# A new order for the first batch's list of steps in a sparse-attention and gated-MLP kernel

## The chip, the cores and the metric

The kernel runs on one core of a Trainium2 chip. The metric is the device time of one execution in microseconds (us), given as the median of three runs. TensorE is called PE here, VectorE DVE, ScalarE ACT, GpSimd POOL; SyncE (SP) does nothing but issue DMAs.

## The reference

For 8 batches of 576 tokens there are 8 attention heads of width 64. Heads 0 to 3 look at the last 32 tokens (local), heads 4 to 7 at every 32nd token back (strided). The heads side by side are x (576 x 512), which goes through a gated MLP:

```python
rel = pos[:, None] - pos[None, :]
mask_local = (rel >= 0) & (rel < stride)                        # stride = 32
mask_strided = (rel >= 0) & (pos[None, :] % stride == pos[:, None] % stride)
attn = softmax(where(mask, q @ k.T / sqrt(D), -1e9)); x = attn @ v
...
h = gelu_tanh(x @ w_in)                                         # 512 -> 1024
u, v = h[..., :512], h[..., 512:]
v_n = (v - mean(v)) / sqrt(var(v) + 1e-06) * g_ln
v_s = einsum('ts,bsd->btd', w_sg, v_n) + b_sg[None, :, None]    # over the tokens
out = x + (u * v_s) @ w_out
```

In the rest of the text "v" with a load or with a head is the attention's v; "the v product" and "the u product" are the two halves of `x @ w_in`.

## The kernel before, in words

**One list of words sets every order.** The kernel has some sixty small step functions. `emit` (L984) walks a string of words and calls one function for each; the class `InOrder` makes every engine run its instructions in the order in which they are issued, and every DMA queue too. A word is a step's name and a number: `SS-:3` is the strided scores of head pair 3. `-` marks the attention of the batch whose MLP is computed, a capital without a mark that of the next batch, `+` the one after it, small letters the MLP, `=` a step that belongs to no batch. `^` sends a step to the other choice of its kind (POOL or DVE, SP or ACT for a DMA, the other pair of PSUM buffers). The string `START` holds batch 0's list; `SECOND`, `LATER`, `CYCLE` and `LAST` hold those of batches 1 to 7.

**What batch 0 has to do beside its own work.** The products are run in two fp32r parts, high and low, so every weight has to be split on the chip. Weights come in 16 halves: 0 to 3 are the v half of `w_in` (one for each head pair of x, that is each 128 rows of the contraction), 4 to 7 the u half, 8 to 15 `w_out`. Each goes through `cl` load (SP), `ck` clip (POOL, `^` DVE), `cc` sign (DVE), `ca` field and `cd` rest (ACT), `ce` add (POOL), `cg` high part (ACT; `wih`, for `w_out` `woh`), `ch` low part (POOL, `^` DVE; `wil`, `wol`). The raw halves of `w_in` sit in the tile `stage`, which has five slots, those of `w_out` in `cs`; between the steps the numbers are in `cv` and `cx`. `w_sg` is transposed on PE in five pieces (`wl` load, `wt` turn, `wh` and `wm` split into `wsh` and `wsl`, `wst` for the last rows and the bias), and a tile `t` (`wo`, `wp`: memset by POOL, then cast by ACT) holds the ones that go with the bias.

**Attention of the first two batches.** `LP` (L439) loads rows of q and k of one head pair into one of four buffers (`rowq`, `rowk`); `TP` (L456) turns them with six PE transposes each, and `TC` (L467) copies the result out of PSUM on ACT (`qT`, `kT`). `SL` is the local scores of a head pair (`sa`, `sr`), `SS` the strided ones (`ss`). The softmax is `MK` mask (DVE), `MX` maximum (DVE), `SB` subtract (POOL, `^` DVE), `EX` exponential (ACT), `SU` sum (DVE), `ML` multiply (POOL, `^` DVE); x = 4 and 5 are the two parts of the local P (tile `sml`), 2 and 3 the strided pairs (`sms`). `PL`, `CL`, `CM` transpose the local P on PE (`ptl`) and copy it out; `VX`, `VY`, `VA` multiply by v (`ol`); `PS`, `CS`, `PV`, `PW` do the same for the strided pairs (`pts`, `os`). `XH` and `XL` write the two parts of x (`xt`), `XR` and `XD` send x out for the residual.

**The products.** `va` to `vd` are the four quarters of the v product for one pair of token tiles; quarter a needs x of head pair 0 and weight half 0, b pair 1 and half 1, and so on. The tail tokens (`v`), layer norm (`l.`), the u product (`u`), the spatial mix (`s`) and the output product (`o`) follow.

Of the kernel before, what the change touches and what calls it, by code (L numbers as in the profile page):

```python
# [22 lines left out]


START = """
cl=:1 LP-:3 cl=:0 LP-:0 TP-:6 mk= TC-^:6 ck=^:1 cl=:8 TP-^:7 cc=:1 ca=:1 mp= wo= wb= cl=:2 TC-:7 cd=:0
SS-^:3 TP-^:0 LZ-:0 cd=:1 TP-^:1 TZ-:0 ck=:0 ce=:1 LP-:1 LP-:2 cg=:1 ml=^ TC-:1 TC-:0 MK-:3 wc= cl=:9 MX-:3
SL-:0 SB-^:3 cl=:3 TP-^:2 ck=^:8 cc=:8 cc=:0 TP-:3 EX-:3 ch=^:1 wp= TZ-:1 ck=:2 MK-:4 SU-:3 MX-:4 TC-:2
SB-^:4 TP-:4 ck=:9 cc=:2 TC-:3 cl=:4 ML-^:3 SL-^:1 MK-:5 LZ-:1 MX-:5 cd=:9 EX-:4 ca=:0 SB-:5 TP-^:5 TC-:5
PS-:3 TZ:1 ce=:0 TC-:4 EX-:5 wd= LP:1 SU-^:4 SU-^:5 ML-:4 LP:0 ca=:2 SS-^:2 MK-^:2 cd=:2 ce=:2 ML-:5 TP^:2  # L30
wl=:1 TP^:3 TZ:0 cg=:0 MX-^:2 TC^:2 cd=^:8 TP:0 cd=:4 cd=:3 ch=:0 TC:3 PL-:5 CS-:3 LV-:0 ck=^:3 ck=^:4
wt=^:1 SB-^:2 CL-:5 cc=:9 cc=^:4 cc=:3 PL-:4 LV-:1 TC:0 EX-:2 TP^:1 cg=:2 CM-:5 ca=:9 CL-^:4 wh=:1 ce=:9
TC:1 VX-^:0 SU-:2 cl=:5 ca=:4 VY-:0 wm=^:1 LV-:3 ML-:2 XHb-:0 SL^:0 XHa-:0 ca=:8 cl=:6 PS-:2 cl=:7 we=^
LV-:2 XLb-:0 VA-:1 XLa-:0 ce=:4 va^:0 XR-:0 CS-:2 va:1 SL:1 XH-:1 XR-:1 XL-:1 vb:1 ca=:3 PV-:3 cd=:6 XD-^:0
MK:0 XD-^:1 ch=:2 PV-^:2 ck=:5 cc=:5 ce=:3 cg=:3 PW-^:3 PW-:2 cd=:5 cl=:13 cg=^:9 LP:3 ce=:8 cg=:4 cl=^:10
ca=:5 LP:2 ck=^:6 ch=:3 vb:0 XH-^:3 XH-:2 ck=^:7 ce=:5 cc=:6 MX:0 XL-:2 XL-:3 cd=:7 XR-:2 XR-:3 vc:0 vd:0
ch=:9 ca=:6 cc=:7 ch=^:4 lg= ce=:6 xt vc:1 LZ:0 cg=:5 cg=:6 cg=:8 g^:0 vd:1 ca=:7 ch=:6 cd=:10 SB^:0 g:1
ch=^:5 ce=:7 v^:2 vh XD-^:3 ls:0 XD-^:2 TP^:7 ls:1 TC:7 cg=:7 TP:6 ck=:13 TP:4 wl=:2 TC:4 vl ch=^:7 lr^:0
cc=:13 lm:0 TC:6 g:2 wl=:4 u^:2 rt LZ:1 u^:0 EX:0 SU:0 LV:0 cd=:13 wt=^:4 ug:2 wl=:0 lr:1 cl=:15 lm^:1 TP:5
lh:0 ll:0 ca=:13 TC:5 wh=:4 u^:1 ls:2 ce=:13 wm=:4 cg=:13 ck=^:10 lm:2 SS^:3 cc=^:10 LV:1 wt=:2 lr:2 MK:3  # L40
ug:0 wt=:0 SS^:2 wl=:3 u:3 ug:1 ca=:10 cl=:14 wh=:0 wh=:2 ML^:0 ce=:10 PL:0 wm=:0 lh^:1 lh:2 ug:3 cl=:11
wt=^:3 cl=:12 MK:2 ck=:15 wm=:2 cg=:10 ll:2 wh=:3 CL:0 ll:1 ch=:10 wm=:3 ck=:14 CM:0 cd=:14 s:1 cc=:14
ch=^:13 LQ+:0 ca=:14 ch=^:8 s:0 cc=:15 VA:0 MX:2 cd=:15 SB^:2 sm:0 ca=:15 VA:1 ce=:14 s:2 sm:1 ce=:15 cg=:14
ck=:11 sh:0 cd=:11 cd=:12 XH:1 cc=:11 MX:3 cg=:15 XL:1 ck=:12 TZ+:0 SB^:3 sh:1 sl:1 ca=:11 ch=:14 sm:2 LQ+:1
ch=^:15 cc=:12 ce=:11 XH:0 cg=^:11 sh:2 sl^:0 ca=:12 ch=^:11 s:3 o:2 sm:3 TZ+:1 XR:1 EX:2 o:0 r o^:1 o^:3
ce=:12 sh:3 sl:3 cg=:12 EX:3 sl^:2 SU:2 ch=^:12 o2:3 SU:3 ML:2 o2:2 PS:2 os:3 LV:2 od^:3 ML:3 XD:1 XL:0 os:2
CS:2 o2^:0 XR:0 LV^:3 LZ+^:1 od:2 PV:2 LV+:1 PW:2 LZ+:0 os:0 PS:3 o2:1 TQ+^:1 XH:2 XR:2 XD^:2 LQ+:2 CS:3
os:1 XD^:0 XL:2 TQ+:0 od^:1 LQ+:3 LV+:0 od^:0
"""
# [991 lines left out]
```

## Time and profile before

| | |
|---|---|
| runs | 555.96, 556.65 and 558.15 us; median 556.65 us |
| profiled execution | span 553.9 us from its first to its last instruction; the page gives no other time of it |
| busy | PE 533.6 us (96%), DVE 397.3, ACT 217.6, POOL 195.8 |
| mean granted clock of TensorE | 0.994 of full speed |

The busy share is a share of the span. PE is the engine to read: outside the first fifty microseconds it has next to no idle time, so a microsecond that PE waits there, or works at a lower clock, is a microsecond of the kernel. In the timeline a row is a run of like instructions: when the first started, how long until the last ended, and how long the engine had been idle before, with what it waited for.

### The profile page before, as it was taken

Reading aid. Unit: us, or ns where it says so; the run is one execution under the profiler, and the core shown is the slowest. Engines: PE = TensorE matmul, PEld = TensorE weight load, DVE = VectorE, ACT = ScalarE, POOL = GpSimd, SP = SyncE. Lnnn points to the kernel's source line nnn. Section 1 sums busy time; section 2 is a strip of 40 time slices with the busy share of each in tenths; the row PEclk is TensorE's granted clock in tenths of the full one; section 3 lists DMA queues with packets and bytes.
Section 4 is the critical chain, followed back from the end, with each engine's and each line's share of the span. In section 5 each row is a group of like instructions: output and inputs, shape, how many; then the busy total and the mean of one; then the engine's idle time right before and its main releaser. Section 6 shows DMA issues by size and latency. Waiting matters only on the chain.

```text
span 553.9 us, 17030 instructions
## 1 busy us (share of the span) xinstructions
PE 533.6 (96%) x7217; PEld 481.2 (87%) x7217; DVE 397.3 (72%) x707; ACT 217.6 (39%) x349; POOL 195.8 (35%) x376
## 2 busy tenths in 40 slices
PE   4869999999999999999999999999999999999997
PEld 3757899878998899988998899988998899988995
DVE  3875997568994499937995399945996399944532
ACT  4665885324440343323531244322631244322320
POOL 7765755404430153303440063302540053302310
PEclk9998999999999999999999999999999999999999
DMA  9898844768756755577446755577455760145002
GB/s 247 210 223 207 177 123 87 158 152 164 159 104 135 158 119 86 109 176 160 80 76 142 167 124 89 100 151 154 102 88 124 177 138 2 44 117 134 1 0 95
DMA packets 253677, 70.07 MB, mean 126 GB/s; under 512 B 237793, under 2 KB 239329, under 8 KB 253602
## 3 DMA queue, kind: packets, MB, share of 16 engines
...
## 4 chain that ended last, share of the span: by engine, by line
PE 85%; DVE 7%; POOL 2%; issue 2%; DMA 1%; SPq 1%; ACT 0%; POOLq 0%; DVEq 0%
PE sg L86 22%; PE o L86 18%; PE v L86 16%; PE u L86 16%; PE ol L86 3%; PE os L86 3%; PE pts L86 2%; PE sa L86 2%; PE ss L86 1%; PE ptl L86 1%; SPq L86 1%; DVE sms L86 1%; DVE cv L86 1%; DVE hv L86 1%; DVE sml L86 1%
## 5 line engine op out<-in xcount | busy, mean ns | idle before, releaser
L86 PE MATMUL sg<-wsh,vg 128*128 128x288 f32 x512 | 113.8, 297 | 0.2 <-DVE vg L86 0.2
L86 PE MATMUL u<-xt,wih 128*128 128x288 f32 x512 | 103.2, 297 | 0.0
L86 PE MATMUL o<-woh,vg 128*128 128x512 f32 x288 | 94.4, 397 | 0.0
L86 PEld LDWEIGHTS sg<-wsh,vg 128*128 128x128 f32 x512 | 85.6, 188 | 0.8 <-DVE vg L86 0.4
L86 PE MATMUL v<-wih,xt 128*128 128x512 f32 x256 | 83.0, 398 | 0.0
L86 PEld LDWEIGHTS u<-xt,wih 128*128 128x128 f32 x512 | 81.7, 188 | 0.7
L86 PE MATMUL u<-xt,wil 128*128 128x288 f32 x256 | 75.6, 295 | 0.4 <-DVE wil L86 0.4
L86 PE MATMUL sg<-wsl,vg 128*128 128x288 f32 x256 | 75.5, 295 | 0.0
L86 PEld LDWEIGHTS o<-woh,vg 128*128 128x128 f32 x288 | 54.1, 188 | 11.1
L86 DVE BATCH_NORM_STATS2 bnst<-hv 128x6 f32<-128x512 f32 (+1 forms) x40 | 27.0, 675 | 44.3 <-ACT hv L86 44.3
L86 PEld LDWEIGHTS v<-wih,xt 128*128 128x128 f32 x256 | 48.7, 190 | 10.5
L86 PE MATMUL o<-wol,vg 128*128 128x512 f32 x144 | 56.2, 390 | 0.0
L86 DVE TENSOR_TENSOR ob<-o,xn 128x512 f32<-128x512 f32 x32 | 20.9, 686 | 44.5 <-PE o L86 39.3
L86 PE MATMUL v<-wil,xt 128*128 128x512 f32 x128 | 50.4, 394 | 0.0
L86 PEld LDWEIGHTS u<-xt,wil 128*128 128x128 f32 x256 | 48.0, 188 | 0.7 <-DVE wil L86 0.7
L86 PEld LDWEIGHTS sg<-wsl,vg 128*128 128x128 f32 x256 | 48.2, 188 | 0.0
L86 ACT CAST vg<-gt 128x576 fp32r<-128x576 f32 (+2 forms) x48 | 22.9, 511 | 57.4 <-DVE gt L86 57.4
L86 ACT COPY pts<-pts 128x576 f32<-128x576 f32 x16 | 10.2, 640 | 74.6 <-PE pts L86 68.2
L86 DVE TENSOR_TENSOR gt<-sg,u 128x576 f32<-128x576 f32 x32 | 23.6, 743 | 19.7 <-PE sg L86 10.0
L86 POOL TENSOR_SCALAR va<-mv 128x2 f32<-128x2 f32 (+1 forms) x16 | 11.0, 687 | 74.4 <-DVE mv L86 74.4
L86 ACT ACTIVATE hv<-v 128x1024 f32<-128x1024 f32 x16 | 16.4, 1027 | 53.0 <-PE v L86 53.0
L86 PEld LDWEIGHTS o<-wol,vg 128*128 128x128 f32 x144 | 27.1, 188 | 4.9
...
## 6 DMA issues: line engine op xcount, KB each, us to landing
...
```

Of the source, the lines that this page charges most:

```text
L86: ins = self.tc.keep_in_program_order(op(*args, **kwargs))
```

## The change

The string `START` is replaced by another order of the same 405 words: none is added, none dropped, none changed, so each step keeps its engine, its queue and its buffers' kind. The other lists and all functions stay. Two lines of the 25 and what stands there now:

```diff
-cl=:1 LP-:3 cl=:0 LP-:0 TP-:6 mk= TC-^:6 ck=^:1 cl=:8 TP-^:7 cc=:1 ca=:1 mp= wo= wb= cl=:2 TC-:7 cd=:0
-SS-^:3 TP-^:0 LZ-:0 cd=:1 TP-^:1 TZ-:0 ck=:0 ce=:1 LP-:1 LP-:2 cg=:1 ml=^ TC-:1 TC-:0 MK-:3 wc= cl=:9 MX-:3
...
+mk= wb= LP-:3 TP-^:7 LP-:0 cl=:1 LP-:2 TP-:6 TP-^:1 TC-:7 TC-^:6 TP-^:0 TZ-:0 mp= wo= cl=:2 ml=^ SS-^:3 ck=:2
+MK-:3 LP-:1 wc= ck=^:1 TC-:1 MX-:3 TC-:0 cc=:1 SB-^:3 SL-:0 TP-:4 MK-:4 LP:0 cl=:3 MX-:4 TP-^:5 SB-^:4 cl=:0
...
```

In the listings below a name carries its batch, its head pair and a running number; where two listings are compared the running numbers differ and mean nothing.

On SP, from the start of the program, the loads stand like this before:

```order
L86 DMA stage_100<-in_moe_w_in_dram 128x2048
L86 DMA rowq_0_3_102<-in_q_dram 96x2x384
L86 DMA rowk_0_3_104<-in_k_dram 96x2x384
L86 DMA stage_100<-in_moe_w_in_dram 128x2048
L86 DMA rowq_0_0_107<-in_q_dram 96x6x64 x2
L86 DMA rowk_0_0_110<-in_k_dram 96x6x64 x2
L86 DMA cs_8_136<-in_moe_w_out_dram 128x1024
L86 DMA stage_100<-in_moe_w_in_dram 128x2048
L86 DMA rowq_0_1_219<-in_q_dram 96x6x64 x2
L86 DMA rowk_0_1_222<-in_k_dram 96x6x64 x2
L86 DMA rowq_0_2_225<-in_q_dram 96x2x384
L86 DMA rowk_0_2_227<-in_k_dram 96x2x384
```

and like this now:

```order
L85 DMA rowq_0_3_115<-in_q_dram 96x2x384
L85 DMA rowk_0_3_117<-in_k_dram 96x2x384
L85 DMA rowq_0_0_126<-in_q_dram 96x6x64 x2
L85 DMA rowk_0_0_129<-in_k_dram 96x6x64 x2
L85 DMA stage_100<-in_moe_w_in_dram 128x2048
L85 DMA rowq_0_2_133<-in_q_dram 96x2x384
L85 DMA rowk_0_2_135<-in_k_dram 96x2x384
L85 DMA stage_100<-in_moe_w_in_dram 128x2048
L85 DMA rowq_0_1_238<-in_q_dram 96x6x64 x2
L85 DMA rowk_0_1_241<-in_k_dram 96x6x64 x2
```

The rows of head pairs 3 and 0 have moved ahead of the first weights, those of pair 2 ahead of pair 1, and the load of `cs` is gone from the front. Further down SP's queue, the load of `w_sg` (whose buffer is the one that held the ones, so that it waits for ACT's cast of them) now has these rows around it; before it stood behind all loads of q and k rows, directly ahead of the loads of v:

```order
L85 DMA stage_100<-in_moe_w_in_dram 128x2048 x2
L85 DMA cs_8_322<-in_moe_w_out_dram 128x1024
L85 DMA wsg_1_331<-in_moe_w_sg_dram 128x576
L85 DMA rowq_1_1_402<-in_q_dram 96x6x64 x2
L85 DMA rowk_1_1_405<-in_k_dram 96x6x64 x2
L85 DMA cs_9_448<-in_moe_w_out_dram 128x1024
L85 DMA v_0_0_481<-in_v_dram 64x9x64
```

On PE, from the last turns ahead of the local P's transposes to the first matmuls of the v product, before:

```order
L86 MATMUL turnq_1_0_510<-ident_72,rowq_1_0_441 128x96 x6
L86 MATMUL ptl_0_4_523<-ident_72,sml_0_329 128x128 x4
L86 MATMUL ptl_0_8_528<-ident_72,sml_0_329 128x128
L86 MATMUL wsgT_1_539<-ident_72,wsg_1_493 128x128 x4
L86 MATMUL wsgT_1_539<-ident_72,wsg_1_493 64x128
L86 MATMUL ptl_0_0_551<-ident_72,sml_0_329 128x128 x4
L86 MATMUL turnk_1_0_564<-ident_72,rowk_1_0_444 128x96 x6
L86 MATMUL ol_0_0_581<-ptl_0_4_574,v_0_0_205 64x32 x32
L86 MATMUL ol_0_0_581<-ptl_0_5_546,v_0_0_205 64x32 x4
L86 MATMUL sa_1_631<-kT_1_0_502,qT_1_0_561 32x64 x36
L86 MATMUL pts_0_2_671<-ident_72,sms0_98 128x100 x8
L86 MATMUL ol_0_1_686<-ptl_0_5_546,v_0_1_393 64x32 x36
L86 MATMUL v_0_0_725<-wih_87,xt_95 128x512
```

and now:

```order
L85 MATMUL ptl_0_0_476<-ident_72,sml_0_298 128x128 x4
L85 MATMUL pts_0_3_487<-ident_72,sms1_99 128x100 x8
L85 MATMUL turnk_1_1_500<-ident_72,rowk_1_1_405 128x96 x6
L85 MATMUL ptl_0_4_536<-ident_72,sml_0_298 128x128 x4
L85 MATMUL ptl_0_8_541<-ident_72,sml_0_298 128x128
L85 MATMUL ol_0_0_547<-ptl_0_4_522,v_0_0_481 64x32 x32
L85 MATMUL ol_0_0_547<-ptl_0_5_545,v_0_0_481 64x32 x4
L85 MATMUL sa_1_613<-kT_1_0_474,qT_1_0_496 32x64 x36
L85 MATMUL ol_0_1_654<-ptl_0_5_545,v_0_1_389 64x32 x36
L85 MATMUL turnq_1_1_701<-ident_72,rowq_1_1_402 128x96 x6
L85 MATMUL v_0_1_725<-wih_87,xt_95 128x512
L85 MATMUL v_0_1_725<-wil_88,xt_95 128x512
```

The first part of the transposed P (`ptl_0_0`) and `w_sg`'s piece are ahead of the last one (`ptl_0_4`); the turn of batch 1's q of pair 1 (`turnq_1_1`) has come down between the second local P V and the v product; the strided transposes (`pts_0_2`) have gone from ahead of the v product to behind its first quarter.

On DVE, at the strided pairs' part of x, before:

```order
L86 SCALAR_TENSOR_TENSOR cv_5_843<-stage_100,cv_5_843 128x512
L86 TENSOR_SCALAR cv_6_808<-stage_100 128x512
L86 TENSOR_SCALAR cv_7_907<-stage_100 128x512
L86 SCALAR_TENSOR_TENSOR cv_6_808<-stage_100,cv_6_808 128x512
L86 TENSOR_REDUCE mx_1_0_911<-sml_1_815 128x18
L86 TENSOR_TENSOR xt_95<-os_0_2_826,xt_95 128x576
L86 TENSOR_TENSOR xt_95<-os_0_3_791,xt_95 128x576
```

and now:

```order
L85 TENSOR_REDUCE mx_1_0_851<-sml_1_791 128x18
L85 TENSOR_SCALAR cv_6_692<-stage_100 128x512
L85 TENSOR_TENSOR sml_1_791<-sml_1_791,mx_1_0_851 128x1152
L85 SCALAR_TENSOR_TENSOR cv_6_692<-stage_100,cv_6_692 128x512
L85 TENSOR_SCALAR cv_7_877<-stage_100 128x512
L85 TENSOR_TENSOR xt_95<-os_0_2_808,xt_95 128x576
L85 TENSOR_TENSOR xt_95<-os_0_3_853,xt_95 128x576
```

The low parts of x of pairs 2 and 3 (`xt<-os`) stand behind the clip of weight half 7 in both; the next batch's maximum and subtraction (`mx_1_0`, `sml_1`) have moved ahead of it, and the sign step of half 5 (`cv_5`) further up.

## Rows read from the trace of the kernel before

**Rows 1.** The page: PE busy; its tenths and clock in 40 slices
```profile
PE 533.6 (96%) x7217; PEld 481.2 (87%) x7217; DVE 397.3 (72%) x707; ACT 217.6 (39%) x349; POOL 195.8 (35%) x376
...
PE   4869999999999999999999999999999999999997
...
PEclk9998999999999999999999999999999999999999
```

**Rows 2.** Waits of PE, 50 to 140 us: total, times, longest
```profile
PE u L86 <- DVE wil L86: 0.4, 1, 0.4
PE os L86 <- DVE sml L86: 0.4, 1, 0.4
PE sg L86 <- DVE vg L86: 0.2, 1, 0.2
```

**Rows 3.** PE, timeline: start, us, operation, count [idle before it <-releaser]
```profile
6.56 1.19 PE L86 MATMUL turnq<-ident,rowq 96*128 96x96 f32 x6 [6.56 <-DMA rowq<-in_q_dram]
...
14.29 1.51 PE L86 MATMUL sa<-kT,qT 64*32 64x64 f32 x72 [1.27 <-ACT qT L86]
...
19.05 0.56 PE L86 MATMUL sa<-kT,qT 64*32 64x64 f32 x22
...
30.80 1.30 PE L86 MATMUL ptl<-ident,sml 128*128 128x128 f32 x5
...
34.70 0.66 PE L86 MATMUL turnk<-ident,rowk 96*128 96x96 f32 x6
35.54 1.25 PE L86 MATMUL ol<-ptl,v 64*64 64x32 f32 x72 [0.18 <-ACT ptl L86]
...
39.41 0.86 PE L86 MATMUL sa<-kT,qT 64*32 64x64 f32 x39 [1.50 <-issue]
40.20 1.59 PE L86 MATMUL pts<-ident,sms 100*128 100x100 f32 x8
41.72 2.15 PE L86 MATMUL ol<-ptl,v 64*64 64x32 f32 x72
43.80 0.79 PE L86 MATMUL v<-wih,xt 128*128 128x512 f32 x1
```

**Rows 4.** DMA queue q1 over 0:36.7 us: packets, MB, share of 16 engines
```profile
q1 hardware_dynamic: 16078, 8.18, 94.5%
```

**Rows 5.** SP, timeline of DMA issues: start, us of issuing
```profile
0.73 0.40 SPq L86 DMA_DIRECT2D stage<-in_moe_w_in_dram  x1
1.18 0.42 SPq L86 DMA_DIRECT2D rowq<-in_q_dram  x1
...
27.91 0.57 SPq L86 DMA_DIRECT2D wsg<-in_moe_w_sg_dram  x1
28.52 6.72 SPq L86 DMA_DIRECT2D v<-in_v_dram  x10
```

**Rows 6.** POOL, timeline: two steps on the local P
```profile
23.33 1.26 POOL L86 TENSOR_TENSOR sml<-sml,mx 128x640 f32<-128x640 f32 x1 [1.80 <-DVE mx L86]
...
28.59 1.26 POOL L86 TENSOR_TENSOR sml<-sml,sr 128x640 f32<-128x640 f32 x1
```

**Rows 7.** ACT, timeline: two casts and copies
```profile
14.84 0.62 ACT L86 CAST t<-ones 33x512 fp32r<-33x512 f32 x1
...
34.90 0.58 ACT L86 COPY ptl<-ptl 128x512 f32<-128x512 f32 x1 [0.44 <-PE ptl L86]
```

**Rows 8.** Windows by stage: us, busy by engine, granted clock, DMA share, GB/s
```profile
0.00:33.00 33.00, 21.35 (x356) 18.32 (x356) 23.07 (x44) 18.62 (x33) 23.82 (x44) 1.00 0.91 227
...
39.67:46.50 6.83, 6.83 (x123) 5.80 (x104) 1.47 (x3) 2.38 (x4) 4.07 (x4) 0.50 0.73 224
46.50:53.00 6.50, 6.11 (x214) 4.80 (x212) 3.85 (x10) 3.00 (x6) 2.75 (x3) 1.00 0.88 176
```

**Rows 9.** Tile stage, 0 to 60 us: duration ns min/median/max, first and last start
```profile
L86 POOL TENSOR_TENSOR cv<-cv,stage x7: 1282/1311/1699, 11.2 to 55.0; 128x512 int32<-128x512 int32 x7
L86 DVE TENSOR_SCALAR cv<-stage x5: 419/551/1499, 5.6 to 51.8; 128x512 f32<-128x512 int16 x5
```

More of the change, by code (lines that the diff above doesn't have):

```diff
@@ L25 @@
 START = """
-cl=:1 LP-:3 cl=:0 LP-:0 TP-:6 mk= TC-^:6 ck=^:1 cl=:8 TP-^:7 cc=:1 ca=:1 mp= wo= wb= cl=:2 TC-:7 cd=:0
-SS-^:3 TP-^:0 LZ-:0 cd=:1 TP-^:1 TZ-:0 ck=:0 ce=:1 LP-:1 LP-:2 cg=:1 ml=^ TC-:1 TC-:0 MK-:3 wc= cl=:9 MX-:3
-SL-:0 SB-^:3 cl=:3 TP-^:2 ck=^:8 cc=:8 cc=:0 TP-:3 EX-:3 ch=^:1 wp= TZ-:1 ck=:2 MK-:4 SU-:3 MX-:4 TC-:2
-SB-^:4 TP-:4 ck=:9 cc=:2 TC-:3 cl=:4 ML-^:3 SL-^:1 MK-:5 LZ-:1 MX-:5 cd=:9 EX-:4 ca=:0 SB-:5 TP-^:5 TC-:5
-PS-:3 TZ:1 ce=:0 TC-:4 EX-:5 wd= LP:1 SU-^:4 SU-^:5 ML-:4 LP:0 ca=:2 SS-^:2 MK-^:2 cd=:2 ce=:2 ML-:5 TP^:2
@@ L31 @@
[L31 to L45, printed above, removed]
@@ L46 @@
-ce=:12 sh:3 sl:3 cg=:12 EX:3 sl^:2 SU:2 ch=^:12 o2:3 SU:3 ML:2 o2:2 PS:2 os:3 LV:2 od^:3 ML:3 XD:1 XL:0 os:2
-CS:2 o2^:0 XR:0 LV^:3 LZ+^:1 od:2 PV:2 LV+:1 PW:2 LZ+:0 os:0 PS:3 o2:1 TQ+^:1 XH:2 XR:2 XD^:2 LQ+:2 CS:3
-os:1 XD^:0 XL:2 TQ+:0 od^:1 LQ+:3 LV+:0 od^:0
+mk= wb= LP-:3 TP-^:7 LP-:0 cl=:1 LP-:2 TP-:6 TP-^:1 TC-:7 TC-^:6 TP-^:0 TZ-:0 mp= wo= cl=:2 ml=^ SS-^:3 ck=:2
+MK-:3 LP-:1 wc= ck=^:1 TC-:1 MX-:3 TC-:0 cc=:1 SB-^:3 SL-:0 TP-:4 MK-:4 LP:0 cl=:3 MX-:4 TP-^:5 SB-^:4 cl=:0
+EX-:3 TC-:5 cl=:8 TP-^:2 wl=:1 TZ-:1 TC-:4 cd=:2 SS-^:2 wd= TP-:3 ca=:1 SU-:3 ML-^:3 MK-^:2 cd=:1 EX-:4 LZ-:1
@@ new lines @@
+wp= ce=:1 TC-:2 TC-:3 SU-^:4 MX-^:2 LP:1 cd=:3 SL-^:1 SB-^:2 cl=:9 TP^:1 MK-:5 TP:0 wt=^:1 ML-:4 TZ:0 PL-:4
+LZ-:0 cg=:1 cd=:0 ck=:0 PS-:3 TC:0 ck=^:8 TP^:3 TC:1 cd=^:8 MX-:5 SB-:5 ck=:9 LV-:0 cc=:2 EX-:2 EX-:5 cc=:0
+CL-^:4 we=^ ca=:0 SU-^:5 CS-:3 ck=^:3 ML-:5 ce=:0 cc=:9 PL-:5 cc=:3 cl=:4 CL-:5 VX-^:0 wh=:1 ca=:9 SU-:2 LV-:1
+CM-:5 cl=:6 ca=:3 VY-:0 cl=:5 TZ:1 cc=:8 cd=:4 ca=:2 TC:3 XHa-:0 wm=^:1 ca=:8 cg=:0 SL^:0 ce=:3 ch=^:1 cl=:13
+VA-:1 ck=^:4 cd=:6 cc=^:4 LV-:2 XHb-:0 ML-:2 XLa-:0 TP^:2 LV-:3 cd=:9 XH-:1 XR-:0 ch=:0 XLb-:0 TC^:2 ce=:8 cg=:3
@@ new lines @@
+XR-:1 ck=:5 va:1 ca=:4 XL-:1 PS-:2 cc=:5 ce=:2 CS-:2 SL:1 va^:0 MK:0 ch=:3 cg=:2 TZ+:1 vb:1 ca=:5 PV-^:2 cl=:7
+PW-:2 XD-^:0 XD-^:1 MX:0 PV-:3 ck=^:6 SB^:0 ce=:9 cg=^:9 ce=:4 cc=:6 XH-:2 ck=^:7 ch=:2 cd=:5 PW-^:3 cl=:11
+XH-^:3 lg= XL-:2 ca=:6 cd=:7 ch=:9 vb:0 XL-:3 EX:0 LP:3 XR-:3 ck=:13 cg=:4 cc=:7 ca=:7 cc=:13 vc:0 ce=:5 cg=:5
+ce=:6 cd=:13 SU:0 XR-:2 XD-^:3 vd:0 xt LZ:0 XD-^:2 ch=^:4 vc:1 g^:0 v^:2 wl=:4 vd:1 cg=:6 LP:2 ce=:7 cg=:7 TP^:7
+vh ch=^:5 ca=:13 ch=^:7 vl g:1 ls:0 TC:7 ch=:6 ce=:13 TP:6 u^:0 lm:0 lr^:0 TC:6 ug:0 g:2 cl=^:10 cd=:10 LZ+:0
@@ new lines @@
+wt=^:4 SS^:3 ls:1 u^:2 wl=:2 u^:1 lr:1 wl=:0 cg=:8 wt=:2 ML^:0 TP:4 ck=:11 wh=:4 wl=:3 lh:0 MK:3 ls:2 wm=:4
+wt=:0 lm:2 LV:0 ug:2 LQ+:1 cg=:13 ll:0 u:3 lm^:1 ug:1 ck=^:10 TC:4 TP:5 wh=:0 cc=^:10 wh=:2 lh^:1 cl=:15 PL:0
+wm=:0 ca=:10 ug:3 wt=^:3 TC:5 SS^:2 lr:2 CL:0 wm=:2 LZ:1 wh=:3 ll:1 ce=:10 wm=:3 cc=:11 ck=:15 lh:2 LQ+:0 ll:2
+MK:2 ca=:11 VA:0 TZ+:0 CM:0 MX:3 MX:2 SB^:3 cl=:12 SB^:2 cd=:11 cd=:15 s:1 EX:3 cl=:14 cg=:10 EX:2 ch=^:13 s:0
+cc=:15 ca=:15 cd=:12 ce=:15 LV:1 ce=:11 sm:1 sm:0 r SU:2 ck=:12 LQ+:3 s:3 ch=:10 cc=:12 ch=^:8 cg=:15 sh:1
@@ L49 @@
+cg=^:11 ck=:14 s:2 cd=:14 ch=^:11 ca=:12 sl:1 sm:3 sh:0 ch=^:15 ce=:12 VA:1 XH:1 XH:0 TQ+^:1 LV:2 sl^:0 sm:2
+cc=:14 ca=:14 o:0 ce=:14 sh:3 sl:3 o:2 XR:0 o^:1 ML:2 cg=:12 rt ch=^:12 SU:3 sh:2 o^:3 sl^:2 XL:1 XL:0 cg=:14
+ch=:14 ML:3 o2^:0 PS:2 o2:1 PS:3 CS:2 os:0 o2:2 XR:1 os:1 od^:0 PV:2 TQ+:0 os:2 XD:1 od^:1 LV^:3 od:2 PW:2
+LZ+^:1 o2:3 LV+:0 XD^:0 XR:2 os:3 od^:3 LV+:1 XH:2 CS:3 LQ+:2 XL:2 XD^:2
 """
```

## The prediction

> **What bounds the kernel now.** I read the busy line and the slices first [rows 1]: PE is busy for 533.6 of 553.9 us, and the only slices of PE below nine tenths at the front are the first four, some 55 us. So PE's work sets the end, and the change, which touches batch 0 alone, can win or lose only where PE waits or runs slowly in that head. The waits behind 50 us come next [rows 2]: in the 90 us from there PE waits 0.4 us for a weight's low part, 0.4 us for masked scores and 0.2 us for the mix's input. Everything behind the start of the v product is therefore one stream, and the time at which that stream starts goes into the span one to one. PE's own timeline [rows 3] gives that start: 43.80 us. The 43 us ahead of it hold four links: the first rows landing (6.56), the second local scores (19.05), the transposes of the local P (30.80) and the two local P V (35.54 and 41.72). The windows [rows 8] add a second limit: PE runs at half clock from 39.67 to 46.5 us, right where the v product begins. That is 0.50, the 1.2 GHz level; ahead of it the clock column reads 1.00, though the same six transposes take 1.19 us at 6.56 and 0.66 us at 34.70 [rows 3], so the engine itself was slow at the start too. Here I go by the durations.
>
> **The change, followed along the path.** What is counted is when the first matmul of the v product can run.
>
> First rows: before, 512 KB of weights and 288 KB of q must land ahead of the first transposes [rows 3, 5]; now the 576 KB of q and k of pair 3 must, since k is turned first. That is 224 KB less. Queue q1 moved 8.18 MB in 36.7 us [rows 4], 223 GB/s, so 1.0 us: 5.6 us instead of 6.56. Four sets of turns at up to 1.19 us and the first strided scores follow, and the first local scores come at about 11.2 us instead of 14.29.
>
> Second local scores: these come later, not earlier. Their rows stand behind another weight half and the rows of pair 2, and on ACT six conversions, casts and exponentials of some 0.6 us each (one of them is in [rows 7]) now stand ahead of the two copies they need. I walk to 21.7 us instead of 19.05, 2.7 us later.
>
> Softmax and transposes of the second local part: POOL's subtraction moves from 23.33 to about 26.0 us. Before, 5.26 us lay from its start to that of the multiply [rows 6], and one 1.3 us conversion add of POOL's stood among them; that add no longer does, so the multiply runs from 30.0 to 31.2 us and the transposes begin at 31.2 instead of 30.80. What was lost upstream is nearly paid back here.
>
> Local P V: before, 4.7 us lay between those transposes and the first P V, because the piece of w_sg and the other half of P came after them. Now both come before. What is left is 1.30 us of transposes, the 0.58 us copy [rows 3, 7] and some 0.2 us of handing over: 33.3 us instead of 35.54. The next batch's first scores wait for DVE's part of w_sg, to about 35.0 us, and take some 1.4. The second P V needs v of pair 1. As many bytes stand ahead of that load as before, and the queue was 94.5% busy to 36.7 us [rows 4], so reordering cannot bring it much forward: 36.2 to 37.8 us. P V takes 1.25 us at the upper level and 2.15 at the lower, the turn behind it 0.66 or 1.19 [rows 3]. The v product can start between 38.1 and 41.0 us. Its second matmul also needs the low part of half 0, which comes on POOL four operations of 1.15 to 1.3 us and their waits after the multiply, about 39.5 us. I take 39.5.
>
> So the terms are:
> - Start of the v product, 43.80 to 39.5: 4.3 us gained (2.8 to 5.7).
> - The strided transposes, 1.59 us at half clock [rows 3], move behind the first quarter. They still cost, at full clock 0.8 us: 0.8 lost from that lead.
> - The wait for masked scores (0.39) goes, since two quarters of v stand between the scores and the strided P V. If they did not cover DVE's masks it would be back: 0.4 lost.
> - The waits of the u product and the mix (0.4 and 0.2) go or stay; I count both, 0.6 gained (0 to 0.6).
> - Low clock: before, the 2.7 us of v product ahead of 46.5 us lost half of that, 1.35 us. If the clock still rises at 46.5, the product now spends 7.0 us at that level and loses 3.5: 2.15 lost.
>
> 4.3 − 0.8 + 0.4 − 2.15 + 0.6 = 2.35 us. The profiled span of 553.9 becomes 551.5. The median of the runs lies 2.75 us above that span (the runs spread over 2.2 us, and a span leaves out what lies around it); I carry that over: 556.65 − 2.35 = 554.3 us. With the bounds of the terms (start 2.8 to 5.7, u and mix 0 to 0.6) it is 552.9 to 556.4.
>
> **The clock term against the notes.** The rows show that PE was at the lower level from 39.67 to 46.5 us after the wait of 1.5 us at 39.41 [rows 3]. They do not show what ended it. The Trainium skill, "TensorE: Matmul & The Clock Gate", section "What's actually happening", says that "the default state is throttled, and activity releases the throttle". By that rule the release would follow the start of the v product, not the time of day, and the low stretch would move forward with it; the term of 2.15 us would fall away. It cuts the other way too: what precedes v still has waits, so the fall itself would not go.
>
> **Rivals.**
>
> The clock follows the work. If the low stretch moves forward by as much as the v product, its loss stays 1.35 us and the gain is 4.5: 552.1. If PE never falls, since the wait of 1.5 us at 39.41 [rows 3] goes, another 1.35: 550.8. For it: the 6.83 us of the window were PE's densest so far, and the rise came within them. Against: the new order has waits of its own at 35 and 36 us. I call this 551.5 us.
>
> POOL or the loads become the bound. POOL has eleven operations from the multiply at 31.2 us to the low part of half 2, by the multiply's 1.26 us [rows 6] 13.9 us, and I walk to 3.4 us of waits between them: 48.5 us. DVE's clip of half 7 reuses a buffer this frees, and the low parts of x of pairs 2 and 3 stand behind that clip; the third quarter waits for them. With 1311 ns as the median of the adds there is room of a microsecond. But the same add took up to 1699 ns and the same clip 419 to 1499 [rows 9]; 0.3 us more on each of eleven is 3.3 us, which leaves a gain of 0 to 1: 556. Against: before, PE had no such wait. The Trainium skill, "GPSIMD Engine Reference", section "1. Specifications", says that POOL shares its SBUF interface with DVE and that they contend when DVE reads two inputs; rows 9 show a spread of that kind, though not its cause.
>
> SP stands still: slower. The load of w_sg waits for ACT's cast of the ones, at 14.84 us before [rows 7] and some 20.6 us in my walk, since it is now behind an exponential and four conversions. Before, that load was issued at 27.91 us [rows 5], long after. Now rows of q and k, half of w_out, all of v of pairs 0 and 1 and a weight half stand behind it in SP's queue. As the queue holds little over, each microsecond that the cast is later than about 20 us makes v of pair 1, and with it the second P V and the v product, as much later. At 26 us it costs 5.5 us and eats the lead of 2.35: 559.8. The point from which it decides is a cast that ends after 23 us. For it: ACT is an in-order engine with four inputs from DVE and POOL ahead of that cast. Against: none of these waits lasts over 2 us in my walk.
>
> **How the numbers follow.** Forecast 0.45 at 554.3; clock with the work 0.2 at 551.5; POOL or DVE as bound 0.23 at 556; SP standing still 0.12 at 559.8. Half a per cent, about what a measurement of this kernel can tell from no change, is 2.8 us: faster means under 553.9, slower over 559.4. Forecast (its range holds 553.9) gives 0.18 of faster, the clock nearly all of its 0.2, the third case 0.01: 0.39. Slower is the greater part of the last, 0.09, and 0.02 of the third: 0.11. No change 0.50. The range leaves out the ends of the clock and of the SP case: 550.5 to 558.3.
>
> **What would show it.** In the changed profile the first transposes start at 5.6 us, the second local scores at 21 to 22, the last set of local transposes at 31, the two P V at 33 and 37, and the v product at 39 to 40; the granted clock is 0.5 until about 46.5. If it rises by 43, the second case holds. If PE waits within the v product for `xt` or `wil`, it is the third; if SP issues the load of w_sg after 23 us and PE waits for the second `v` load past 39, it is the fourth. My forecast is wrong if the v product starts after 41.5 us, or starts at 39.5 and the lead is gone by the u product.

## The result, and the profile after

| | before | after |
|---|---|---|
| runs, us | 556.42 (median of 4) | 562.99 (562.38 to 565.72, 4 runs) |
| profiled span, us | 553.9 | 560.9 |

The ratio of the runs is 1.0125, with a 95% interval of 1.0097 to 1.0153. The change makes the kernel slower by 1.25%, some 7 us. That is above the range given (550.5 to 558.3), and the side with the smallest chance.

The page after, in the lines that answer to [rows 1] (busy us by engine, tenths of PE and granted clock in 40 slices):

```profile
PE 535.2 (95%) x7217; PEld 482.3 (86%) x7217; DVE 405.1 (72%) x707; ACT 214.2 (38%) x347; POOL 195.8 (35%) x376
...
PE   5589899979999999999999999999999999999997
...
PEclk9658999999999999999999999999999999999999
```

The same 7217 matmuls cost PE only 1.6 us more, so some 5.4 of the 7.0 us are waits. DVE's same 707 instructions cost 7.8 us more: some of them have become slower. The clock is low in the second to the fourth slice, from 17 us on. The waits that PE has from 50 to 140 us, where [rows 2] had three with 1.0 us in all (and leave out a fourth, 0.69 us at `os` with no engine as its releaser):

```profile
PE os L85 <- ACT pts L85: 1.3, 1, 1.3
PE turnq L85 <- ACT hv L85: 1.2, 1, 1.2
PE pts L85 <- DVE xt L85: 1.0, 1, 1.0
PE v L85 <- DVE xt L85: 0.9, 1, 0.9
PE o L85 <- DVE ob L85: 0.8, 1, 0.8
PE o L85 <- DVE gt L85: 0.8, 1, 0.8
PE o L85 <- DVE wol L85: 0.3, 1, 0.3
PE sg L85 <- PE ol L85: 0.2, 1, 0.2
```

They come to 6.5 us, most of them put down to DVE. Two lie ahead of the u product (`v`, `turnq`); the others, but for the mix's 0.2, lie between 106 and 125 us, in batch 0's output product and batch 1's strided part beside it. The timeline of PE for the head, which answers to [rows 3]:

```profile
5.01 1.19 PE L85 MATMUL turnk<-ident,rowk 96*128 96x96 f32 x6 [5.01 <-DMA rowk<-in_k_dram]
...
11.21 1.51 PE L85 MATMUL sa<-kT,qT 64*32 64x64 f32 x72
...
22.00 0.56 PE L85 MATMUL sa<-kT,qT 64*32 64x64 f32 x22 [1.85 <-ACT kT L85]
...
28.42 1.30 PE L85 MATMUL wsgT<-ident,wsg 128*128 128x128 f32 x5 [2.78 <-DMA wsg<-in_moe_w_sg_dram]
...
34.08 1.11 PE L85 MATMUL ptl<-ident,sml 128*128 128x128 f32 x4 [1.21 <-POOL sml L85]
35.87 0.48 PE L85 MATMUL ptl<-ident,sml 128*128 128x128 f32 x1 [0.68 <-ACT ptl L85]
36.27 2.15 PE L85 MATMUL ol<-ptl,v 64*64 64x32 f32 x72
...
39.91 2.14 PE L85 MATMUL ol<-ptl,v 64*64 64x32 f32 x72
41.99 1.22 PE L85 MATMUL turnq<-ident,rowq 96*128 96x96 f32 x6
44.15 0.77 PE L85 MATMUL v<-wih,xt 128*128 128x512 f32 x1 [0.95 <-DVE xt L85]
```

The v product starts at 44.15 us, not at 39.5. The walk held up to the second local scores (22.00 us against 21.7). In this execution, set against the walk, 2.9 us were lost between there and the transposes of the second local P, which came at 34.08 instead of 31.2; another 1.8 were lost behind the second P V, which together with the turn runs at the lower level. What POOL and DVE did ahead of the transposes (POOL's two steps on the local P answer to [rows 6]):

```profile
28.32 1.63 POOL L85 TENSOR_TENSOR sml<-sml,mx 128x640 f32<-128x640 f32 x1 [0.95 <-DVE mx L85]
31.25 1.09 POOL L85 TENSOR_SCALAR cx<-cs 128x256 f32<-128x256 int16 x1 [1.30 <-DMA cs<-in_moe_w_out_dram]
32.77 1.26 POOL L85 TENSOR_TENSOR sml<-sml,sr 128x640 f32<-128x640 f32 x1 [0.43 <-DVE sr L85]
33.98 1.47 POOL L85 TENSOR_TENSOR cv<-cv,stage 128x512 int32<-128x512 int32 x1
```

```profile
27.13 0.38 DVE L85 TENSOR_SCALAR cx<-cs 128x256 f32<-128x256 int16 x1 [1.94 <-DMA cs<-in_moe_w_out_dram]
27.43 0.80 DVE L85 TENSOR_REDUCE mx<-sml 128x10 f32<-128x640 f32 x1
28.16 2.34 DVE L85 SCALAR_TENSOR_TENSOR cv<-stage,cv 128x512 f32<-128x512 int16 x2
...
34.23 1.77 DVE L85 SCALAR_TENSOR_TENSOR cv<-stage,cv 128x512 f32<-128x512 int16 x1
```

DVE's clip of weight half 8 stands ahead of the maximum of the local scores and waits 1.94 us for its load. POOL's clip of half 0 waits for its load too (1.76 us) and ends at 27.37, so the subtraction could not have started before that. It starts at 28.32 instead of 26.0, and the multiply behind it at 32.77 instead of 30.0. DVE's sign step, 0.69 us where nothing disturbs it, took 1.77 us beside POOL's add. Over the head the eight sign steps have a mean of 1190 ns; the same group before had 697 ns.

The windows by stage (columns as in [rows 8]) show DVE with next to no gap ahead of the v product (15.88 of 16.15 us), and the lower level of the clock throughout the stretch:

```profile
28.00:44.15 16.15, 12.85 (x250) 11.29 (x251) 15.88 (x24) 10.44 (x23) 11.81 (x10) 0.50 0.74 190
44.15:47.40 3.25, 3.25 (x10) 2.59 (x11) 2.78 (x3) 0.78 (x2) 3.25 (x3) 0.50 0.78 239
47.40:53.00 5.60, 5.60 (x170) 4.62 (x171) 3.91 (x8) 1.98 (x4) 5.51 (x7) 0.98 0.80 178
```

Where the 7.0 us of span are can be read from first matmuls in the two timelines:

| first matmul of | before, us | after, us | later by |
|---|---|---|---|
| v product | 43.80 | 44.15 | 0.35 |
| strided P V | 50.96 | 51.83 | 0.87 |
| u product | 63.26 | 66.15 | 2.89 |
| output product | 101.30 | 103.63 | 2.33 |
| batch 1's v product | 115.82 | 121.18 | 5.36 |
| its tail tokens | 127.99 | 134.69 | 6.70 |

So 0.35 us are ahead of the v product, 2.5 between it and u, and 4.1 behind the start of u (490.7 to the end before, 494.75 after).

### The profile page after: what moved, and what is told of

Read it like the earlier page. It is cut to its first block, busy times and chain, and to the rows that moved or that the text cites. A ratio compares the mean times of both kernels' runs of the same rounds, so it can differ in the third digit from the quotient of the medians.

```text
span 560.9 us, 17031 instructions
## 1 busy us (share of the span) xinstructions
PE 535.2 (95%) x7217; PEld 482.3 (86%) x7217; DVE 405.1 (72%) x707; ACT 214.2 (38%) x347; POOL 195.8 (35%) x376
## 4 chain that ended last, share of the span: by engine, by line
PE 84%; DVE 6%; DMA 3%; ACT 3%; SPq 1%; issue 1%; ACTq 0%; POOL 0%; DVEq 0%
PE sg L85 21%; PE u L85 18%; PE o L85 16%; PE v L85 16%; PE ol L85 3%; PE os L85 2%; PE ss L85 2%; PE sa L85 2%; PE pts L85 2%; DVE cv L85 2%; DMA rowk<-in_k_dram 2%; SPq L85 1%; DMA xd<-xs 1%; PE ptl L85 1%; DVE xs L85 1%
## 5 line engine op out<-in xcount | busy, mean ns | idle before, releaser
L85 POOL MEMSET v<- 32x128 f32 x16 | 3.2, 198 | 82.9 <-PE os L85 65.7
```

Of the source, the lines that this page charges most:

```text
L85: ins = self.tc.keep_in_program_order(op(*args, **kwargs))
```

## The experiments

Each kernel was timed against the kernel before on the same chip; a ratio above 1 is slower than before. Words in the diffs are those of `START`. "Control" is the changed kernel again (E14, below): 1.0089 [1.0071, 1.0108].

**E1 and E2: which half of the list costs?** E1 puts the old end behind the new head, E2 the new end behind the old head; the cut is at the first u words.

```diff
 E1: new list up to the first u word (without cl=:11 and TZ+:1)
-    new list from there
+    old list from there
 E2:
-    new list up to u^:0
+    old list up to u^:2
     new list from there
```

> The new order up to the first word of the u product (without the load of weight half 11 and one memset of the third batch), and behind it the remaining words in the old order. Theory (two separate losses: 2.9 us are lost by the start of the u product, because DVE and POOL are full with conversions there, and about 3.8 us behind it, because the rest of the list waits for DVE and ACT in the output stage): only the first loss is left, some 559.5 us, and PE's waits of 0.8 to 1.3 us in the output stage are gone. Rival (the waits of the output stage are the late head, handed on): they stay, some 562.5 us. Rival (the tail alone loses): as before, 556.4.

> The old order up to the first word of the u product, and behind it the remaining words in the new order. Theory (two separate losses): the second is left, 556.4 + 3.8 = 560.2 us, with the u product starting at 63 us as before and PE waiting in the output stage. Rival (the late head is handed on): 556.4, no such waits. Rival (the tail alone loses): 563.

E2 took 1.0101 [1.0073, 1.0128], some 5.6 us, with waits of the kind seen above. From u to the end it has 495.3 us, as after (494.75; before 490.7), so the end costs 4.7 us in this profile. The other 1.9 us of its span are ahead of u (65.20 us, before 63.26), in an execution of the old head that ran at the lower level to 49 us. E1 took 1.0143 [1.0121, 1.0164], but the place where the two lists meet has waits of its own (a turn waits 3.2 us at 68.44 for DVE's layer norm, another 1.4 for ACT), so its total says nothing of the head. It does show that the old end, run behind a late head, has none of the output stage's waits.

**E3: the head without w_out.** The conversion steps of `w_out` that the new head has go behind the u product's start.

```diff
-cl=:8 ... cl=:9 ... ck=^:8 ... cd=^:8 ... ck=:9 ... cc=:9 ... ce=:13 (21 words, among the steps of the head)
 u^:0
+cl=:8 cl=:9 ck=^:8 cd=^:8 ck=:9 cc=:9 ... ce=:13
```

> The new order, but all conversion steps and loads of w_out's halves (8 and up) that stand ahead of the u product are moved, in their order, to directly behind its first word. Five DVE instructions, seven of POOL and one wait for a load of w_out leave the head. Theory (DVE and POOL hold up the head: DVE is busy 15.9 of the 16.2 us ahead of the v product, its sign steps stretched from 0.7 to up to 1.8 us where POOL runs beside them): the last maximum of the local P ends near 26 instead of 28.2 us, the v product starts 1.5 to 3 us earlier than 44.15, the wait of 0.9 us in the third quarter shrinks. Rival (the low clock of PE sets the head): the v product starts within 0.5 us of 44.15. Rival (loads of v set it): the same. The total depends on what the moved steps cost behind u; no theory rests on it.

1.0318 [1.0286, 1.0349]. The v product started at 41.23 us, but the steps now held ACT and DVE ahead of batch 1's scores, and PE waited 10.8 us for `qT` at 76.86. Put there, the work costs more than it saves in the head; another place was not tried.

**E4 and E8: the two causes upstream.** E4 takes the waiting clip from ahead of the maximum, E8 gives POOL's steps on the second local P to DVE.

```diff
 E4:
-ck=^:8 TP^:3 TC:1 ... MX-:5 SB-:5
+TP^:3 TC:1 ... MX-:5 ck=^:8 SB-:5
 E8:
-ck=:0   SB-:5   ML-:5
+ck=^:0  SB-^:5  ML-^:5
```

> The new order with one word moved: DVE's clip of weight half 8 stands behind the maximum of the last part of the local P instead of ahead of it, so that DVE no longer waits 1.9 us there for the load of w_out. Theory (a chain of DVE and POOL work sets the head): the maximum ends at 26 instead of 28.2, but POOL's clip of half 0 runs to 27.4, so the subtraction comes 0.9 us earlier; of that 0 to 0.9 us reach the v product, 562.1 to 563. Rival (this wait alone is what made the head late): 2 us, 561.

> The new order with three steps moved from POOL to DVE, in their places: the clip of weight half 0 and the subtraction and multiplication of the last part of the local P. POOL loses 4.8 us of work ahead of the v product, DVE gets some 2. Theory (POOL and DVE together hold up the head, POOL's long instructions lying in the chain and stretching DVE's beside them): the last local transposes start at 32 to 33 instead of 34.08 us, the v product at 42 to 43 instead of 44.15, and the whole takes 561 to 562. Rival (DVE alone is full: 15.9 of 16.2 us): the v product starts 1 to 2 us later, 564 to 565. Rival (clock or loads): no change.

E4 took 1.0115 [1.009, 1.0139], transposes at 33.24 and the v product at 43.04; E8 took 1.0141 [1.0114, 1.0167], 33.14 and 43.47. Neither is better than the kernel after (1.0125) or the control, and links earlier by 0.7 to 1.1 us are less than the same head differs by from one execution to the next (E14, below). In E4 the maximum is done at 25.8 us, but POOL's clip of half 0, which waits 2.0 us for its load, holds the subtraction until 27.5: the waiting clip on DVE was only part of the delay. E8 is clear on one thing, the stretched sign steps. DVE, then POOL, in E8:

```profile
27.65 1.29 DVE L85 SCALAR_TENSOR_TENSOR cv<-stage,cv 128x512 f32<-128x512 int16 x2
...
38.45 3.47 DVE L85 SCALAR_TENSOR_TENSOR cv<-stage,cv 128x512 f32<-128x512 int16 x1
```

```profile
38.09 1.34 POOL L85 TENSOR_TENSOR sms<-sms,sr 100x576 f32<-100x576 f32 x1
39.39 1.29 POOL L85 TENSOR_TENSOR wil<-cv,wih 128x512 fp32r<-128x512 f32 x1
40.64 0.73 POOL L85 TENSOR_TENSOR cx<-cx,cs 128x256 int32<-128x256 int32 x1
41.34 2.40 POOL L85 TENSOR_SCALAR cv<-stage 128x512 f32<-128x512 int16 x1
```

The two signs that POOL no longer accompanies take 0.65 us each. The one at 38.45 met POOL's queue instead and ended at 41.92, after three of POOL's instructions had gone by. The collision was moved, not removed.

**E5 and E6: the cut elsewhere.** E5 keeps the new list to the first quarter of v, E6 the old list from the third mix on.

```diff
 E5: new list up to va:1
-    new list from there
+    old list from there
 E6: new list up to the third mix
-    new list from there
+    old list from there
```

> The new order up to the first quarter of the v product, the remaining words behind it in the old order. Theory (the front loses little by itself, since its v product starts at 44.15 against 43.80 us; the rest is lost by the order behind it): the u product starts at 64 to 64.5 us instead of 63.26, the output stage has none of the five waits, and the whole takes 557 to 558 us. Rival (the crowded front is what is paid for, by DVE and POOL work that it leaves undone): the u product starts at 65.5 or later and the whole takes 560 or more.

> The new order up to the third product of the spatial mix (without two loads or memsets of batch 2), the remaining words in the old order; the cut lies behind the u product, so that the seams of the first experiment fall away. Theory (the order of the output stage has waits of its own, 4.1 us less the 0.7 of before): the five waits of PE between 105 and 126 us are gone, the u product still starts near 66, and the whole takes 563 - 3.5 = 559.5 us. Rival (the waits are the late head handed on): they stay, 563.

E5 took 1.0027 [1.001, 1.0044]: the new front, with the strided transposes ahead of the v product as in the old list, costs 1.5 us. With E2's 1.01% that is 1.28%, about the whole loss, but the sum settles less than it seems: neither run has the new order between v's first quarter and u, where the profile after has its waits of 0.87 and 1.18 us, and against the control (1.0089) E2 alone is the whole loss. In E5's profile, one of the slowest of its 12 runs (560.84 us, median 558.38), u starts at 67.04 us, as the rival had it, while the median is near the theory's. E6 took 1.0217 [1.0195, 1.0239]: the output stage's waits are gone but for 0.3 us, but a load of v was issued too late at the seam and the local P V waited 5.35 and 1.61 us for it. It settles nothing. E9 joined E6 with E4 and E8 and waited there as well, 1.0199 [1.0177, 1.0221].

**E10, E11, E13 and E14: taking POOL out of DVE's way in the output stage.** E10 gives two gate multiplications to DVE; E11 also moves ACT's copy of strided P and a turn; E13 adds E4's clip and moves the clip of half 7 behind the low parts of x, which the third quarter waits for. E14 changes nothing.

```diff
 E10, E11, E13:
-sl^:0 ... sl^:2
+sl:0 ... sl:2
 E11, E13:
-TQ+:0 os:2 ... XH:2 CS:3
+os:2 TQ+:0 ... CS:3 XH:2
 E13 (and E4's line):
-XH-:2 ck=^:7 ch=:2 ... vb:0 XL-:3
+XH-:2 ch=:2 ... vb:0 XL-:3 ck=^:7
```

> The new order with two steps of the output stage moved from POOL to DVE in their places: the low parts of gated columns 0 and 2. They are the two POOL instructions beside which DVE's low parts of w_out took 1.48 and 1.95 us instead of 0.4. Theory (DVE's instruction is held until POOL's beside it is done): the two low parts of w_out take 0.4 us each again, DVE has 1.5 us of new work and 2.6 less of waiting, and PE's waits at 106, 111 and 113 us (0.8, 0.3, 1.0) shrink by about 1.2 in all: 561.8 us. Rival (DVE is simply full): those waits grow by 0.7 to 1.5 in all, 564 us. Rival (the stretched rows are an artefact of the record): durations stay.

> As the run before it, and two words moved in the output stage: ACT's copy of the strided transposes of pair 3 ahead of the high part of x of pair 2 (which waits for DVE and through it for a DMA's buffer), and DVE's turns of batch 2's first pair behind the third output addition. Theory (each wait of the output stage has its own cause in the order): the waits at 119.7 (0.8) and 125.3 (1.25) go as well, 2 us more than the run before it, 560 us. Rival (the waits replace one another): within 0.7 us of the run before it.

> The mended tail of the second run, with DVE's clip of weight half 8 behind the last local maximum and its clip of half 7 behind the low parts of x of pairs 2 and 3. Theory (the loss is the sum of named waits): 1.1 us of the head and 0.9 of the third quarter go on top: 558 us. Rival (the front's waits replace one another): 559.5 to 560.

> The new order unchanged, as the control for the run that follows on the same chip and as one more execution of its head (the v product started between 41.2 and 44.2 us in four executions of that same head). Any theory: 1.0 to 1.5% slower than the old order, with the five waits of the output stage at 0.8, 0.3, 1.0, 0.8 and 1.25 us. If the head's executions vary as widely as the runs so far say, the v product starts anywhere in 41 to 44.5 us and the waits are unchanged.

E10 took 1.0076 [1.0054, 1.0098], E11 1.0073 [1.0047, 1.0098], E13 1.0105 [1.0075, 1.0135], E14 1.0089 [1.0071, 1.0108]: no difference from the control that these intervals can tell. E14 is the kernel after once more, which took 1.0125 the first time: ratios 0.4% apart can belong to the same kernel. E14 also shows how much the head differs by itself: the same waits of the output stage, but the clip of half 8 found its load there and DVE's maximum began at 25.27 us, the transposes at 31.90 and the v product at 41.99. DVE's two low parts of `w_out` at the output stage, as groups of E10 and of the kernel after (count | busy us, mean ns):

```profile
L85 DVE TENSOR_TENSOR wol<-cxl,woh 128x256 fp32r<-128x256 f32 x2 | 1.7, 836 | 0.0
```

```profile
L85 DVE TENSOR_TENSOR wol<-cxl,woh 128x256 fp32r<-128x256 f32 x2 | 3.4, 1716 | 0.0
```

The same group had 388 ns before. The collision is half gone in E10 (0.41 and 1.26 us), and its wait with it, but PE now waits for the gates, since DVE makes them (waits of PE in E10):

```profile
PE o L85 <- DVE vg L85: 2.0, 2, 1.1
...
PE o L85 <- DVE ob L85: 0.8, 1, 0.8
```

In E13 the wait of the third quarter went and the turn behind it waited 2.2 us instead of 1.2.

**E15, E17 and E18: DVE's own order.** E15 moves the low part of half 15, turns and a store's transpose out of the way of what PE waits for; E17 adds to it three POOL steps given to DVE; E18 moves only the sign and field of half 12, which wait for a late clip, behind the gates.

```diff
 E15, E17:
-ch=^:15 ce=:12 VA:1 XH:1 XH:0 TQ+^:1 LV:2 sl^:0 sm:2
+ce=:12 VA:1 XH:1 XH:0 LV:2 sl^:0 sm:2 ch=^:15 TQ+^:1
 (XR:0 behind ch=^:12; E11's second pair of lines)
 E17:
-ML:2  sl^:0  sl^:2
+ML^:2 sl:0   sl:2
 E18:
-cc=:12 ... ca=:12 sl:1 sm:3 sh:0
+sl:1 sm:3 cc=:12 ca=:12 sh:0
```

> The new order with five words moved inside the output stage, no engine changed: on DVE the last gate multiplication ahead of the turns of batch 2's second pair and of a low part of w_out, the low part of half 12 ahead of a store's transpose, the third output addition ahead of the turns of batch 2's first pair; on ACT the copy of the strided transposes of pair 3 ahead of the high part of x of pair 2. Theory (PE's waits there come from what stands ahead on DVE and ACT): from the start of the u product to the v product of batch 1 it takes 53 to 53.7 us instead of 55.0 (52.6 in the old order), the waits at 106, 111 and 113 us go, and the whole is 2 to 3 us faster than the control. Rival (the waits replace one another, as when the two low gates went to DVE): 54.5 or more, within 0.7 us of the control.

> The tail order of the run with five moved words, and three POOL steps of the output stage on DVE in their places: the low parts of gated columns 0 and 2 and the multiplication of the strided P of pair 2. Beside these DVE's low parts of w_out took 0.97 to 2.73 us instead of 0.4. Theory (a DVE instruction that starts beside a POOL instruction is held until that one, and the next if it follows at once, has ended; that is what the output stage of the new order loses): the low parts take 0.4 us each although DVE has 2.2 us more of its own work, and from the start of the u product to the v product of batch 1 it takes 52.8 to 53.8 us (new order 55.0, five moved words 58.0, old order 52.6). Rival (DVE is too full there whatever runs beside it): 55 or more.

> The changed order with one sign step and one field step of w_out's half 12 moved behind the last gate multiplication. Theory (DVE's queue order in the output stage): DVE's sign of that half stood idle for about 2.5 us for POOL's clip, which itself waited for a late load, and the gate multiplications queued behind it. With the sign behind them the wait of 0.77 us at the output product goes, first u to batch 1's first v product takes 53.0 to 53.7 us instead of 55.0, and the kernel is 1 to 2 us faster than the unchanged new order (ratio to before 1.006 to 1.008, where that order had 1.009 and 1.0125). Rival (DVE is full there, and waits replace one another): the 0.77 us appears at another product, first u to batch 1's v stays at 54.5 us or more, ratio 1.009 or above.

E15 took 1.0155 [1.0133, 1.0176]. The wait for the gate's input is gone, but the low part now starts in the midst of two POOL instructions (DVE, then POOL, in E15):

```profile
107.18 2.73 DVE L85 TENSOR_TENSOR wol<-cxl,woh 128x256 fp32r<-128x256 f32 x1
```

```profile
106.59 1.68 POOL L85 TENSOR_TENSOR sms<-sms,sr 100x576 f32<-100x576 f32 x1
108.24 1.39 POOL L85 TENSOR_TENSOR vg<-gt,vg 128x576 fp32r<-128x576 f32 x1
```

It ended at 109.91, 0.28 us after the second of them, and PE waited 1.7 us for it. In E17 those POOL steps are DVE's, and the same instruction is short (DVE, then POOL, in E17):

```profile
108.99 0.41 DVE L85 TENSOR_TENSOR wol<-cxl,woh 128x256 fp32r<-128x256 f32 x1
```

```profile
108.78 1.21 POOL L85 TENSOR_TENSOR wol<-cxl,woh 128x256 fp32r<-128x256 f32 x1 [1.00 <-ACT woh L85]
```

POOL is not idle beside it: a low part of its own had started 0.21 us earlier, and this time POOL's instruction was the long one (1.21 us; 0.73 in E10). The clean case is the low part of half 15. It took 1.48 us at 102.53 in the kernel after, beside POOL's gate multiplication, and 0.41 us with POOL idle, in E10 (99.62) and in E17 (104.43). So POOL is what stretches it. E17 differs from E15 by those three steps alone and took 1.008 [1.0056, 1.0105], with the intervals apart: in E15's order the collision cost time. Against the control it won nothing: PE waited 1.9 us for a gate that DVE made late, and u to batch 1's v took 54.5 us, between the theory (up to 53.8) and the rival (55). E18 took 1.0091 [1.0063, 1.0119]; the wait of 0.77 us for `gt` became one of 0.91 us for POOL's `vg`, and u to batch 1's v took 55.1 us, as in the kernel after (55.0). That is what the rival said: the waits replace one another.

**E12 and E16: one step in the old list.** E12 is the kernel before with DVE's copy of the last transposed piece of the local P moved ahead; E16 adds the high and low part of half 7 moved forward.

```diff
 E12, E16 (old list):
-CL-:5 cc=:9 ... cg=:2 CM-:5
+CL-:5 CM-:5 cc=:9 ... cg=:2
 E16:
-vh ... ls:1 TC:7 cg=:7 ... ch=^:7
+cg=:7 vh ... ch=^:7 ls:1 TC:7
```

> The old order with one word moved: DVE's copy of the last transposed piece of the local P ahead of three sign steps (1.7 us) that stood in front of it. PE waits 0.96 us for that copy at 34.21 us before. Theory (a chain of DVE work sets the start of the v product in the old order too): that wait goes, both local P V and the v product come up to 1 us earlier, 0.1 to 0.2% faster than before. Rival (v of pair 1 or the waits behind set it): no change.

> The old order with the copy of the last piece of P first, as in the run that was 0.22% faster, and with ACT's high and DVE's low part of weight half 7 moved ahead of the second layer-norm statistics. In that run the u product waited 1.69 us for this low part, which ended at 65.3 as in the old order, so that the earlier v product was given back there. Theory (a chain of conversions on ACT and DVE is a floor under the u product): the wait goes, 0.4 to 0.5% faster than the old order, some 554 us. Rival (something else then holds the mix or the layer norm): as the run with one move, 0.2%.

E12 took 0.9978 [0.9964, 0.9992], E16 0.9973 [0.9955, 0.9991]: both are faster than the kernel before, by about a quarter of a per cent, in 12 runs each; E16 is not told apart from E12. E12 also tests the statement that the start of v goes into the span one to one. Its v product starts 3.0 us earlier than before. Most of that is not the copy's. The wait of 0.96 us for it went, but PE then waited 1.30 us for ACT's copy, and the first local P V came 0.45 us later than before. Behind it the wait of 1.50 us at 39.41 [rows 3] is gone, and PE was at the upper level from 33.2 us on (the second P V took 1.25 us instead of 2.15). This is what the stream made of it (PE in E12):

```profile
40.81 0.50 PE L85 MATMUL v<-wih,xt 128*128 128x512 f32 x1
...
44.85 0.73 PE L85 MATMUL v<-wih,xt 128*128 128x512 f32 x2 [1.90 <-issue]
```

and its waits from 40 us:

```profile
PE v L85 <- issue: 1.9, 1, 1.9
PE u L85 <- DVE wil L85: 1.7, 1, 1.7
```

PE lost 1.9 us in the product itself and 1.7 us at u, waiting for `wil`; at the mix nothing of the lead was left (83.31 us against 83.33). The wait of 1.9 us has no releaser on record, like the one of 1.50 us that stood ahead of the product before; it may be the same wait in another place, which was not tested. The profile, of a slow execution (556.53 us, median 555.48), does not account for the gain of 1.3 us in the runs. In E16 the wait for `wil` is gone and the mix starts at 82.51.

## Why the prediction was wrong

**The step that failed first is "Everything behind the start of the v product is therefore one stream, and the time at which that stream starts goes into the span one to one."** It was read from the waits of the old order [rows 2], but the list `START` runs on to the end of batch 0 and all of it was put in a new order. The prediction costed no step behind the mix. From the start of u on, the new order takes 4.1 us more in the profile, by waits between 106 and 125 us, and the new end by itself costs 1.01% in the runs (E2). The statement is also false inside the old order: in E12 a lead of 3.0 us at the v product had become 1.3 at the u product (61.98 against 63.26) and nothing at the mix. Two readings that this step rests on were short: only the first three slices of PE are below nine tenths, not four, and [rows 2] leave out the wait of 0.69 us at 112 us.

**The second was the lead, "I take 39.5".** It was a walk along single durations, and two things in it failed. The waits for loads ahead of the subtraction were not in it, DVE's clip of half 8 and POOL's of half 0: where these loads are late, as in the kernel after, the transposes are 2.9 us late, and still 2.0 with the clip of half 8 out of the way (E4). Where they are in time, the walk holds up to there, and still the v product is 2 us later than 39.5. PE, in E18, whose head is that of the kernel after:

```profile
31.60 1.11 PE L85 MATMUL ptl<-ident,sml 128*128 128x128 f32 x4 [1.18 <-POOL sml L85]
...
33.80 2.15 PE L85 MATMUL ol<-ptl,v 64*64 64x32 f32 x72
...
39.74 1.22 PE L85 MATMUL turnq<-ident,rowq 96*128 96x96 f32 x6
41.67 0.76 PE L85 MATMUL v<-wih,xt 128*128 128x512 f32 x1 [0.71 <-ACT qT L85]
```

The P V take 2.15 us and more, the turn 1.22, where 1.25 and 0.66 are those of the upper level: the prediction named both durations and took 39.5 between them, but the whole stretch was low. And the product waits for its inputs, 0.7 here, 0.95 in the kernel after. Over nine executions of this head (after, E1, E6, E10, E11, E14, E15, E17, E18) the v product began at 41.2 to 44.15 us. For the old head there are two, 43.80 and E2's 44.81. The lead is some 1.5 us on the mean, and no execution had 4.3.

**Terms.** The strided transposes cost 1.2 us, mostly at half clock, where 0.8 was allowed. The wait for masked scores (0.39) went, as predicted. In place of the 0.6 us saved at u and the mix, the third quarter waited 0.87 us and a turn 1.18: 1.5 us lost net of the old waits. The clock term of 2.15 us did not arise, since the product had no lead to spend at the lower level: it ran 2.7 us there before and, with the strided transposes apart, 2.7 us after. Where there was a lead the term did arise: in E10 the product started at 41.21 us and the level rose at 46.66, so that 5.45 us of the stream (the first quarter, the strided transposes, scores) went by at the lower level, against 2.7 before.

**Rivals.** "The clock follows the work" is half borne out. The rise came at 47.57, 44.83 and 46.66 us with the v product starting at 44.15, 41.99 and 41.21 (after, E14, E10): it is not fixed to 46.5, and it does not keep a distance from the product either. That PE would not fall was wrong: it was low from 16.85 us on in the kernel after, through a stretch in which it was busy for 12.85 of 16.15 us; the rule of the Trainium skill, "TensorE: Matmul & The Clock Gate", section "What's actually happening", that activity releases the throttle, did not show itself in that stretch. "SP stands still" was wrong: ACT's cast ended at 20.75 us and SP issued the load of w_sg at 20.77, as walked. That load still came late on PE (2.78 us waited at 28.42).

"POOL or the loads become the bound" had the mechanism, and named the place. In the third quarter the low parts of x do stand behind the clip of half 7, and that clip is stretched beside POOL (DVE, then POOL, in the kernel after):

```profile
54.55 1.54 DVE L85 TENSOR_SCALAR cv<-stage 128x512 f32<-128x512 int16 x1
56.02 1.41 DVE L85 TENSOR_TENSOR xt<-os,xt 128x576 fp32r<-128x576 f32 x2
```

```profile
54.32 2.92 POOL L85 TENSOR_TENSOR cv<-cv,stage 128x512 int32<-128x512 int32 x2 [0.85 <-ACT stage L85]
```

What it had wrong is the size. It priced the spread of [rows 9] at 0.3 us on each POOL operation and let it eat the gain at most; the stretch is mostly on DVE's side, 1 to 2.8 us on one instruction, and it recurs in the output stage. There POOL was busy for 9.5 of the 18 us from 100 to 118, where before it was 4.7: four more of its steps stand in that stretch now.

**What stays open.** POOL's collisions were shown to stretch DVE's instructions (E8, E15, E17), and DVE's queue order to hold the gates (E18), but taking away any of them did not bring the 4 us back. No single cause of the end's loss is shown; what is shown is that it belongs to the new end (E2), and that the waits for `gt`, for `wol` and in the third quarter, once removed, were followed by others (E18, E10, E13). What the stretch between the v product's start and u costs in the runs is not shown by itself. Nor is the gain of E12 and E16 traced to one wait.
